# Moving the output stores to SyncE, spreading the second attention and loading batch 2 earlier, in a retention and MLP kernel

## The chip, the cores and the metric

The kernel runs on one core of a Trainium2 chip. The metric is device microseconds of a whole execution. Times are medians of several executions; the span, which the profile gives, is some 2 us shorter than the time of its execution. All profiled executions are in the fast state. The record marks one other execution of e12 and three of the kernel before beside it as slow (over 1.5% above the fastest of their kernel); the ratios leave these out. Executions of one kernel lie within some 2% of each other, so a single span can be off by as much.

Engine names as in the profile: PE is TensorE, DVE VectorE, ACT ScalarE, POOL GpSimd, SP or SPq SyncE and its queue. "DMA share" is the mean busy share of the core's 16 DMA engines. In these profiles it can pass 1 (1.41 in the kernel before, from 84.26 to 92.58 us). The granted PE clock is the share of full clock that PE was given, 1 for all of it.

## The reference

```python
scores = (q @ k.T) / sqrt(64)                 # q, k, v: 8 batches, 8 heads, 576 tokens, 64
ret = scores * Dmat                           # Dmat[h, i, j] = gamma_h ** (i - j) for i >= j, else 0
x = heads_side_by_side(ret @ v)               # 8 x 576 x 512
u = x + (x.T @ U @ V).T                       # U: 576 x 32, V: 32 x 576
out = u + relu(u @ w1) @ w2                   # w1: 512 x 2048, w2: 2048 x 512
```

## The kernel before

Two batches form a pair of nine chunks of 128 tokens; the fifth chunk (XC) is shared by the two batches. A batch goes through a "front" (load, cast, transpose, attention, mixer) and an MLP of two matmul stages, y1 and y2. In the profile, `psc` are the attention scores, `qT` and `kT` the transposed q and k, `ut` a tile of mixed tokens that goes into the MLP, `uT` its transpose, and `o_sb` a finished output tile. The program is one list of instructions, sorted by an estimate of PE's time: the front of a later batch is laid between the MLP matmuls of an earlier one. Each engine has its own part of the list, and in the trace of this kernel it works that off in order: a store on ACT was issued at 174.26 us, after the landing of a v load at 174.19, and the relu behind it, which PE had waited for 3.2 us, came at 174.85.

SyncE issues all loads of q, k, v and x and all transposes by DMA, in that order of the program. ACT does copies and relus, and in this kernel it also issues the output stores:

```python
    STQ = nc.scalar
    # ... (load of k and v for one chunk; kv_f has 4 buffers)
    f = stage.tile([P, 2, H, D], FP32, tag="kv_f", name="kv_f", bufs=4)
    for j, dram in ((0, k), (1, v)):
        nc.sync.dma_start(
            out=f[:, j], in_=dram[g, :, t0:t0 + P, :].rearrange("h s d -> s h d")
        )
    # ... (end of y2 of one tile of 128 tokens; o_sb has 3 buffers, J = 4, P = 128)
    o_sb = osb_pool.tile([P, dm], FP32, tag="o_sb", name="o_sb")
    nc.vector.tensor_tensor(out=o_sb, in0=self.ps[i], in1=self.st["u", c], op=ALU.add)
    row0 = (self.p * NCH + c) * P
    dst = out_flat[row0:row0 + P, :]
    if c != XC:
        dst = dst.rearrange("(p j) d -> j p d", j=J)
    stores.append(lambda: STQ.dma_start(out=dst, in_=o_sb))
    if len(stores) > 1:
        stores.pop(0)()
```

Two things in it matter later. A store is emitted one tile late, when the next tile's addition has been emitted. And, except for the XC tile, the rows of `o_sb` are a permutation of the tokens (token 4p+j lies in partition 32j+p), so the destination of the store is written as three nested dimensions: 4 values of j, 32 of p, 512 elements.

Of the kernel before, what the change touches and what calls it, by code (L numbers as in the profile page):

```python
# [11 lines left out]
AF = mybir.ActivationFunctionType  # L12
# [29 lines left out]
def kernel(  # L42
# [11 lines left out]
    nc = tc.nc  # L54
# [4 lines left out]
    R = moe_U.shape[1]  # L59
    P = 128  # L60
    HALF = 64
    NHP = H // 2
# [14 lines left out]
    NG = B  # L77
    AHEAD = 2
    SKEW = 0.65
    FILL1 = (0.33, 0.85)  # L80
    LOAD2 = (0.75, 0.12)
    FRONT2 = 0.15
    LAG = 2
    WARM = (4, 2, 2, 2, 2, 2)

    STQ = nc.scalar
    scale = 1.0 / math.sqrt(D)
    lng = [math.log(1.0 - 2.0 ** (-5.0 - h)) for h in range(H)]
    out_flat = out.rearrange("b s d -> (b s) d")
# [22 lines left out]
    def big(name, dtype=FP32, shape=None):  # L112
        return ps_big.tile(shape or [P, 512], dtype, tag="ps_big", name=name)
# [106 lines left out]
    def put_u(par):  # L220

        f, t, m0 = ((U_fA, U_A, 0), (U_fB, U_B, 1))[par]
        un = mix_pool.tile([P, 4, R], BF16, tag="un", name="un")
        nc.vector.tensor_copy(out=un, in_=f[:, m0:m0 + 4, :])
        ps = big("psu")
        nc.tensor.matmul(
            ps[:, 0:4 * R], perm, un.rearrange("p m r -> p (m r)"), start=True, stop=True
        )
        nc.vector.tensor_copy(
            out=t[:, m0:m0 + 4, 0:R],  # L230
            in_=ps[:, 0:4 * R].rearrange("p (m r) -> p m r", r=R),
        )

    def put_mixer_a():
        put_u(0)
        nc.vector.tensor_copy(out=U_A[0:HALF, 4, 0:R], in_=U_fA[0:HALF, 4, :])
        put_v(V_A, 0, 0)

    def put_mixer_b():
        put_u(1)  # L240
        nc.vector.tensor_copy(out=V_A[0:R, 4 * P:S], in_=V_nat[:, 4 * P:S])
        nc.vector.tensor_copy(out=U_B[HALF:P, 0, 0:R], in_=U_fB[HALF:P, 0, :])
        put_v(V_B, P, HALF)
        nc.vector.tensor_copy(out=V_B[0:R, HALF:P], in_=V_nat[:, 0:HALF])
# [8 lines left out]
    def load_w1(fbs):  # L253
        dmas = []
        for fb in fbs:
            cols = slice(fb * W1B, (fb + 1) * W1B)
            dmas.append(
                nc.gpsimd.dma_start(
                    out=w1_sb[:, :, cols],
                    in_=moe_w_ch1[:, cols].rearrange("(c p) f -> p c f", p=P),  # L260
                )
            )
        return dmas[-1]
# [51 lines left out]
            )  # L315
        sts[p]["kv_f", m + 5 * par] = f

    def cast_kv(g, m):
        cast_v(g, m)
        cast_k(g, m)  # L320

    def cast_v(g, m):
        p, c = g // 2, m + 5 * (g % 2)
# [2 lines left out]
        scale_v(t[:, 1], f[:, 1], c)  # L326
        sts[p]["k", c], sts[p]["v", c] = t[:, 0], t[:, 1]

    def cast_k(g, m):
        st, c = sts[g // 2], m + 5 * (g % 2)  # L330
        nc.vector.tensor_copy(out=st["k", c], in_=st["kv_f", c][:, 0])  # L331

    def load_x(p, part=None):

# [13 lines left out]
    def cast_x(p, part=None):  # L348
        cast_xv(p, part)
        cast_xqk(p, part)  # L350
# [16 lines left out]

    def cast_xqk(p, part=None):
        f, rows = sts[p]["x_f"], x_rows(part)
        nc.vector.tensor_copy(out=sts[p]["x3"][rows, 0:2], in_=f[rows, 0:2])  # L370

    def pair_cols(t, hp):
        return t[:, 2 * hp:2 * hp + 2, :].rearrange("p h d -> p (h d)")
# [2 lines left out]
    class Front:  # L376
# [57 lines left out]
        def TX(self, n=128):  # L434
            t = self.st["qk", XC]
            xT = x3_pool.tile([P, 2, NHP, P], BF16, tag="xT", name="xT")
            self.st["xT"] = xT
            if not self.pe_t:
                nc.sync.dma_start_transpose(
                    out=xT.rearrange("p j hp i -> p (j hp) i"),  # L440
                    in_=t.rearrange("p j h d -> p (j h d)"),
                )
                return
            ps = big("psx", BF16, [P, 2, NHP, P])
            for j in (1, 0):
                for hp in range(NHP):
                    nc.tensor.transpose(
                        ps[:, j, hp, 0:n], pair_cols(t[0:n, j], hp), ident[0:n, 0:n]
                    )
            if self.quick:  # L450
                self.copy(xT[:, 1, :, 0:n], ps[:, 1, :, 0:n])
                self.copy(xT[:, 0, :, 0:n], ps[:, 0, :, 0:n], act=False)
            else:
                self.copy(xT, ps)

# [292 lines left out]
    def first_front():  # L748
        fr = Front(0, True, quick=True)
        st = fr.st  # L750
        dummy = big("dummy")

        def warm(n):

            for _ in range(n):
                nc.tensor.matmul(
                    dummy.rearrange("p (a b) -> p a b", b=P), ident,
                    ident[:, None, :].to_broadcast([P, 4, P]), start=True, stop=True,
                )

        warm(WARM[0])
        cast_q(0, quick=True)
        cast_kv(0, 0)
        fr.TQ()
        fr.TK(0)
        cast_kv(0, 1)
        fr.SC(0)
        fr.ST(0)
        warm(WARM[1])
        fr.TK(1)  # L770
        fr.RV(0)
        cast_kv(0, 2)
        fr.SC(1)
        fr.ST(1)
        warm(WARM[2])
        fr.TK(2)
        fr.RV(1)
        put_mixer_a()
        w1a = load_w1(range(0, 2))
        cast_x(0, 0)  # L780
        fr.SC(2)
        fr.ST(2)
        fr.MA(0)
        warm(WARM[3])
        fr.TX(HALF)
        fr.RV(2)
        fr.MA(1)
        cast_kv(0, 3)
        load_w1(range(2, 4))
        fr.SC(XC, HALF, None)  # L790
        warm(WARM[4])
        fr.TK(3)
        fr.MA(2)
        fr.ST(3)
        fr.SC(3, cross=None)
        fr.CR(XC, HALF)
        fr.RV(XC, HALF, rows=slice(0, HALF))
        fr.uT_tile()
        uT = st["uT", 0]
        acc = [  # L800
            ps_s.tile([P, 512], FP32, tag="ps_s", name="uT_s"), big("uT_b"),
            big("uT_c"),
            ps_sc.tile([P, 2, 512], FP32, tag="ps_sc", name="uT_sc")[:, 0, :],
        ]

        def x_t(c, ccs=range(NCC)):
            for cc in ccs:
                nc.tensor.matmul(
                    acc[cc][:, c * P:(c + 1) * P],
                    st["x", c][:, cc * P:(cc + 1) * P], ident,  # L810
                    start=(c == 0), stop=False, skip_group_check=True,
                )

        for c in range(3):
            x_t(c, range(3))
        fr.CR(3)
        fr.RV(3)
        fr.MA(4, 3)
        for c in range(3):
            x_t(c, range(3, 4))  # L820
        fr.MA(3, 3)
        x_t(3)
        for cc in range(NCC):
            nc.tensor.matmul(
                acc[cc], st["a_sb", 0][:, cc * P:(cc + 1) * P], V_A[:, 0:4 * P],
                start=False, stop=True, skip_group_check=True,
            )
            fr.copy(uT[:, cc, :], acc[cc], act=cc % 2 == 1)
        return fr, w1a


    def loads_of(g):

        if g >= NG:
            return []
        ld = [(load_q, g)] + [(load_kv, g, m) for m in range(4)]
        cs = [(cast_q, g)] + [(cast_kv, g, m) for m in range(4)]
        if g % 2 == 0:
            ld.append((load_x, g // 2))
            cs.append((cast_x, g // 2))  # L840
        n = len(ld)
        steps = []
        for i in range(n + LAG):
            def step(i=i):
                if i >= LAG:
                    f = cs[i - LAG]
                    f[0](*f[1:])
                if i < n:
                    f = ld[i]
                    return f[0](*f[1:])  # L850
            steps.append((step,))
        return steps

    with tc.manual_schedule(engines={PE, POOL, SPQ, DVE, ACT}):
# [22 lines left out]
        for m in range(4):  # L877
# [3 lines left out]
                cast_xv(0, 1)  # L881
            if m == 2:
                w2_part = load_w2()
        fill = [(0, put_mixer_b)] + [(216, lambda c=c: first.MH(c)) for c in range(2)]
        fill += [(0, lambda: cast_k(1, 0)), (0, lambda: cast_xqk(0, 1))]
        fill += [(0, lambda: cast_q(1, (0, 1))), (0, lambda: cast_q(1, (2, 3)))]
        fill += [(216, lambda c=c: first.MH(c)) for c in range(2, 4)]
        casts = [(cast_k, 1, m) for m in range(1, 4)]
        fill += Front(1, True).items(casts, x_alone=True)

# [4 lines left out]
        def spread(items, lo, hi):  # L895
            tot = sum(c for c, _ in items) or len(items)
            at = 0.0
            for c, f in items:
                events.append((lo + (hi - lo) * at / tot, f))
                at += c if tot != len(items) else 1  # L900
# [10 lines left out]
        def at(g, share):  # L911
            return starts[g] + share * (starts[g + 1] - starts[g])

        spread(fill, at(0, FILL1[0]), at(0, FILL1[1]))
        lo2 = [(0, f) for f, in loads_of(2)]

        def first_load(f=lo2[0][1]):
            tc.add_manual_dep(f().ins, w2_part.ins.name, SYNC)

        lo2[0] = (0, first_load)  # L920
        spread(lo2, at(0, LOAD2[0]), at(1, LOAD2[1]))
        lo = at(1, FRONT2)
        fronts = {g: Front(g, False) for g in range(2, NG)}
        for g in range(2, NG):
# [37 lines left out]
```

## Time and profile before

| | before |
|---|---|
| time | 371.01 us (368.33 to 373.85) |
| span of the profiled run (an execution of 373.52 us) | 371.7 us |
| PE busy | 332.2 us, 89% |
| first y1 / first y2 | 31.18 / 59.70 us |
| first scores of batch 2 | 92.58 us |
| from there to the end of the span | 279.1 us |

The profiled execution took 2.5 us more than the median, so spans of other kernels look that much better beside it. I split the span at the first scores of batch 2, because up to there the kernel fills its pipeline, and after it the same pattern runs batch after batch.

One more reading of this kernel is needed below. It is the busy time in stretches (columns: stretch, length, then PE, weight loads, DVE, ACT, POOL, granted PE clock, DMA share, GB/s), in the tail, when all work is done and only the last store is under way:

```profile
364.80:365.80 1.00, 0.00 (x0) 0.00 (x0) 0.00 (x0) 0.00 (x0) 0.00 (x0) 1.00 0.26 100
```

This store, which has the whole machine to itself, moves 100 GB/s and keeps 0.26 of 16, so about four, DMA engines busy. I overlooked this line when I predicted.

### The profile page before, as it was taken

The page shows a single profiled execution, that of the slowest core. Times are in us where ns is not written, and L with a number is a line of the kernel's source. Part 1 is how long each engine was busy: PE and PEld are TensorE (multiplying, and loading weights), DVE is VectorE, ACT ScalarE, POOL GpSimd, SP SyncE. Part 2 cuts the span into 40 slices and gives each one's busy share as a digit, 9 for nine tenths or more (in the row PEclk, how much of TensorE's full clock was granted, in tenths as well). Part 3 has the DMA queues.
Part 4 walks back from the last instruction along what each step waited for, and adds up shares of the span by engine and source line. Part 5 has one row for each costly group of instructions (what it writes and reads, how often), then busy time and mean ns, then how long its engine had stood idle before and what let it go on. Part 6 is the DMA issues. An engine that isn't in the chain of part 4 may idle for free.

```text
span 371.7 us, 6390 instructions
## 1 busy us (share of the span) xinstructions
PE 332.2 (89%) x2606; PEld 184.4 (50%) x2642; DVE 154.8 (42%) x245; ACT 146.2 (39%) x284; POOL 56.2 (15%) x81
## 2 busy tenths in 40 slices
PE   3778687898997999996999999998999999999991
PEld 1454244445663554444665554545765544467540
DVE  5672546652853661463412662264424532210020
ACT  3425453135553126512574135504662156148200
POOL 8640620310130111112112001201100000000000
PEclk9989969999999999999899999999999999999997
DMA  8999899939999999988994347999902200110112
GB/s 208 194 200 243 175 176 266 203 83 180 192 173 222 167 118 178 212 131 168 159 212 91 78 110 157 218 112 159 112 15 67 56 23 0 50 65 2 56 48 64
DMA packets 127149, 49.66 MB, mean 134 GB/s; under 512 B 110192, under 2 KB 122480, under 8 KB 127120
## 3 DMA queue, kind: packets, MB, share of 16 engines
q1 hardware_dynamic: 117440, 35.48, 58.9%
q10 hardware_dynamic: 5456, 9.59, 9.1%
q0 software_dynamic: 4224, 4.19, 7.1%
q8 instruction: 20, 0.33, 0.5%
q14 instruction: 9, 0.07, 0.1%
HBM read 36.92 MB, written 9.44 MB: 125 GB/s over the span
## 4 chain that ended last, share of the span: by engine, by line
PE 67%; DMA 13%; SPq 7%; DVE 6%; ACT 3%; issue 2%; ACTq 0%; POOL 0%; DVEq 0%; POOLq 0%
DMA kv_f<-in_v_dram 5%; DMA kT<-kv 4%; PE psc L487 3%; SPq L313 3%; PE po L535 2%; DVE q_bf L299 2%; PE pu L600 2%; PE ph L581 2%; DMA q_f<-in_q_dram 2%; PE pss L465 2%; DVE ret L523 2%; SPq L401 2%; SPq L340 1%; PE psa L564 1%; DMA x_f<-in_v_dram 1%
## 5 line engine op out<-in xcount | busy, mean ns | idle before, releaser
L699 PEld LDWEIGHTS <-w_sb 128*128 128x128 bf16 x768 | 73.0, 99 | 52.7 <-issue 7.4
L303 POOL TENSOR_TENSOR kv<-kv_f,vscale 128x512 bf16<-128x512 f32 x32 | 34.3, 1071 | 190.4 <-DMA kv_f<-in_v_dram 133.6
L523 DVE TENSOR_TENSOR ret<-psc,tri 128x1024 bf16<-128x1024 f32 x32 | 39.1, 1223 | 33.0 <-PE psc L487 32.9
L470 ACT ACTIVATE s_sb<-pss 128x512 bf16<-128x512 f32 x32 | 19.1, 596 | 61.1 <-PE pss L465 36.1
L587 DVE TENSOR_TENSOR ut<-ph,xt 128x512 bf16<-128x512 f32 x36 | 24.4, 688 | 44.8 <-PE ph L581 44.8
L543 DVE TENSOR_TENSOR xt<-po,qscale 128x512 bf16<-128x512 f32 (+1 forms) x37 | 25.5, 689 | 21.1 <-PE po L535 20.9
L388 ACT ACTIVATE uT<-pu 128x512 bf16<-128x512 bf16 x32 | 18.9, 596 | 25.8 <-PE pu L600 21.3
L535 PEld LDWEIGHTS <-ret 128*128 128x128 bf16 x288 | 12.7, 100 | 10.5 <-DVE ret L523 5.9
L331 DVE CAST kv<-kv_f 128x512 bf16<-128x512 f32 x32 | 14.6, 462 | 4.2 <-DMA kv_f<-in_k_dram 4.1
L487 PE MATMUL psc<-qT,kT 64*128 64x128 bf16 x256 | 13.4, 227 | 2.9 <-DMA kT<-kv 1.7
L487 PEld LDWEIGHTS <-kT 64*128 64x128 bf16 x256 | 7.6, 97 | 15.5 <-issue 11.2
L600 PEld LDWEIGHTS <-ut 128*128 128x128 bf16 x128 | 9.6, 98 | 11.1 <-issue 3.2
L600 PE MATMUL pu<-ident,ut 128*128 128x128 bf16 x128 | 12.4, 219 | 3.0 <-ACT uT L388 2.6
L535 PE MATMUL po<-kv,ret 128*128 128x64 bf16 x256 | 13.2, 196 | 1.7 <-DVE ret L523 1.4
L299 DVE CAST q_bf<-q_f 128x512 bf16<-128x512 f32 x30 | 13.4, 509 | 3.0 <-DMA q_f<-in_q_dram 3.0
L709 PEld LDWEIGHTS <-y_4028 128*128 128x128 bf16 x80 | 7.8, 98 | 9.3
L465 PE MATMUL pss<-kv 128*128 128x128 bf16 x112 | 11.5, 229 | 0.8 <-ACT s_sb L470 0.7
L465 PEld LDWEIGHTS <-kv 128*128 128x128 bf16 x112 | 8.8, 102 | 5.9 <-issue 1.0
L410 PE MATMUL psq<-ident,q_bf 128*128 128x128 bf16 x32 | 4.1, 308 | 7.7 <-DVE q_bf L299 7.6
L709 PEld LDWEIGHTS <-y_1084 128*128 128x128 bf16 x80 | 7.2, 98 | 6.7
L709 PEld LDWEIGHTS <-y_3202 128*128 128x128 bf16 x80 | 7.2, 98 | 6.6
L709 PEld LDWEIGHTS <-y_2209 128*128 128x128 bf16 x80 | 7.2, 98 | 6.6
(585 smaller groups left out, 590.4 us busy)
## 6 DMA issues: line engine op xcount, KB each, us to landing
out_dram<-o_sb ACTq DMA_DIRECT2D x36, 256.0 KB
q_f<-in_q_dram SPq DMA_DIRECT2D x8, 1024.0 KB
kv_f<-in_k_dram SPq DMA_DIRECT2D x32, 256.0 KB
kv_f<-in_v_dram SPq DMA_DIRECT2D x32, 256.0 KB
w_sb<-in_moe_w_ch_dram POOLq DMA_DIRECT2D x8, 512.0 KB, 8.3
x_f<-in_k_dram SPq DMA_DIRECT2D x8, 128.0 KB
x_f<-in_q_dram SPq DMA_DIRECT2D x8, 128.0 KB
x_f<-in_v_dram SPq DMA_DIRECT2D x8, 128.0 KB
```

The source lines that it names most:

```text
L299: nc.vector.tensor_copy(out=dst, in_=src)
L303: nc.gpsimd.tensor_tensor(out=dst[rows], in0=src[rows], in1=vscale[rows, c, :, None].to_broadcast([n, H, D]), op=ALU.mult,)
L465: nc.tensor.matmul(pss[:, hp, :], pair_cols(st["k", c], hp), pair_cols(vt, hp), start=(first and hp == 0), stop=True, skip_group_check=True,)
L470: nc.scalar.activation(out=s_sb, in_=pss, func=AF.Copy)
L487: nc.tensor.matmul(psc[0:n, hl, hp, 0:n], kT[pb:pb + HALF, hp, 0:n], qTv[pb:pb + HALF, hp, 0:n], start=True, stop=True,)
L523: nc.vector.tensor_tensor(out=ret[0:n].rearrange("p (hp hl) i -> p hl hp i", hl=2)[:, :, :, 0:n], in0=psc[0:n, :, :, 0:n], in1=mask[0:n, N ...
L535: nc.tensor.matmul(po[0:n, hl, hp * D:(hp + 1) * D], ret[:, h, 0:n], vt[:, h, :], start=((c == 0 or not cross) and hp == 0), stop=True, sk ...
L543: nc.vector.tensor_tensor(out=st["x", c][rows].rearrange("p (hp hl d) -> p hl hp d", hl=2, d=D), in0=po[rows, :, 0:NHP * D].rearrange("p h ...
L587: nc.vector.tensor_tensor(out=ut, in0=ph, in1=st["x", c], op=ALU.add)
L600: nc.tensor.transpose(pu[:, cc, :], self.st["u", c][:, cc * P:(cc + 1) * P], ident)
L699: nc.tensor.matmul(ps[:, 0:n], w1_sb[:, cc, f * P:(f + 1) * P], uT[:, cc, t0:t0 + n], start=(cc == 0), stop=(cc == NCC - 1),)
L709: nc.tensor.matmul(self.ps[i], self.y1[:, f, i * P:(i + 1) * P], w2_sb[:, f, :], start=(f == 0), stop=(f == NF - 1),)
```

## The change

Its intent: shorten the start (casts of k and x on ACT), fill PE's idle time in the first y1 with the second attention, load batch 2 in one go ahead of the first store, and take the stores off ACT, whose relus had waited behind them. The core of the diff, with cuts marked:

```diff
-    FILL1 = (0.33, 0.85)
-    LOAD2 = (0.75, 0.12)
-    FRONT2 = 0.15
+    FILL1 = (0.2, 0.8)
+    LOAD2 = 0.62
+    CAST2 = (0.78, 0.12)
+    FRONT2 = 0.2
-    STQ = nc.scalar
+    STQ = nc.sync
 ... (put_u is split: its cast comes early, its matmul and copy later)
+        if quick:
+            nc.scalar.activation(out=st["k", c], in_=st["kv_f", c][:, 0], func=AF.Copy)
 ... (the same for batch 0's x cast and one xT copy; first_front reordered)
-        fill = [(0, put_mixer_b)] + [(216, lambda c=c: first.MH(c)) for c in range(2)]
-        fill += [(0, lambda: cast_k(1, 0)), (0, lambda: cast_xqk(0, 1))]
+        fill = [(216, lambda c=c: first.MH(c)) for c in range(2)]
         fill += [(0, lambda: cast_q(1, (0, 1))), (0, lambda: cast_q(1, (2, 3)))]
         fill += [(216, lambda c=c: first.MH(c)) for c in range(2, 4)]
+        fill += [(0, lambda: cast_k(1, 0)), (0, lambda: cast_xqk(0, 1))]
 ...
+        events.append((at(0, 0.05), put_mixer_b))
...
-        spread(lo2, at(0, LOAD2[0]), at(1, LOAD2[1]))
+        def load_2():
+            i = load_q(2)
+            tc.add_manual_dep(i.ins, w2_part.ins.name, SYNC)
+            for m in range(4):
+                load_kv(2, m)
+            load_x(1)
+
+        events.append((at(0, LOAD2), load_2))
+        cast_2 = [lambda hp=hp: cast_q(2, (hp,)) for hp in range(NHP)]
+        cast_2 += [lambda m=m: cast_kv(2, m) for m in range(4)] + [lambda: cast_x(1)]
+        spread([(0, f) for f in cast_2], at(0, CAST2[0]), at(1, CAST2[1]))
```

More of the change, by code (lines that the diff above doesn't have):

```diff
@@ L224, in put_u, with rest, put_mixer_a @@
         nc.vector.tensor_copy(out=un, in_=f[:, m0:m0 + 4, :])
-        ps = big("psu")
-        nc.tensor.matmul(
-            ps[:, 0:4 * R], perm, un.rearrange("p m r -> p (m r)"), start=True, stop=True
-        )
-        nc.vector.tensor_copy(
-            out=t[:, m0:m0 + 4, 0:R],
-            in_=ps[:, 0:4 * R].rearrange("p (m r) -> p m r", r=R),
-        )
-    def put_mixer_a():
-        put_u(0)
+        def rest():
+            ps = big("psu")
+            nc.tensor.matmul(
+                ps[:, 0:4 * R], perm, un.rearrange("p m r -> p (m r)"),
+                start=True, stop=True,
+            )
+            nc.vector.tensor_copy(
+                out=t[:, m0:m0 + 4, 0:R],
+                in_=ps[:, 0:4 * R].rearrange("p (m r) -> p m r", r=R),
+            )
+        return rest
+    def put_mixer_a(u_rest):
+        u_rest()
         nc.vector.tensor_copy(out=U_A[0:HALF, 4, 0:R], in_=U_fA[0:HALF, 4, :])
@@ L239, in put_mixer_b @@
     def put_mixer_b():
-        put_u(1)
+        put_u(1)()
         nc.vector.tensor_copy(out=V_A[0:R, 4 * P:S], in_=V_nat[:, 4 * P:S])
@@ L316, in load_kv, with cast_kv @@
         sts[p]["kv_f", m + 5 * par] = f
-    def cast_kv(g, m):
+    def cast_kv(g, m, quick=False):
         cast_v(g, m)
-        cast_k(g, m)
+        cast_k(g, m, quick)
     def cast_v(g, m):
@@ L327, in cast_v, with cast_k @@
         sts[p]["k", c], sts[p]["v", c] = t[:, 0], t[:, 1]
-    def cast_k(g, m):
+    def cast_k(g, m, quick=False):
         st, c = sts[g // 2], m + 5 * (g % 2)
-        nc.vector.tensor_copy(out=st["k", c], in_=st["kv_f", c][:, 0])
+        if quick:
+            nc.scalar.activation(out=st["k", c], in_=st["kv_f", c][:, 0], func=AF.Copy)
+        else:
+            nc.vector.tensor_copy(out=st["k", c], in_=st["kv_f", c][:, 0])
     def load_x(p, part=None):
@@ L369, in cast_xqk @@
         f, rows = sts[p]["x_f"], x_rows(part)
-        nc.vector.tensor_copy(out=sts[p]["x3"][rows, 0:2], in_=f[rows, 0:2])
+        dst, src = sts[p]["x3"][rows, 0:2], f[rows, 0:2]
+        if part == 0:
+            nc.scalar.activation(out=dst, in_=src, func=AF.Copy)
+        else:
+            nc.vector.tensor_copy(out=dst, in_=src)
     def pair_cols(t, hp):
@@ L451, in TX @@
                 self.copy(xT[:, 1, :, 0:n], ps[:, 1, :, 0:n])
-                self.copy(xT[:, 0, :, 0:n], ps[:, 0, :, 0:n], act=False)
+                self.copy(xT[:, 0, :, 0:n], ps[:, 0, :, 0:n])
             else:
@@ L764, in first_front @@
         fr.TQ()
+        u_rest = put_u(0)
         fr.TK(0)
-        cast_kv(0, 1)
+        cast_kv(0, 1, True)
         fr.SC(0)
+        put_mixer_a(u_rest)
         fr.ST(0)
@@ L771, in first_front @@
         fr.RV(0)
-        cast_kv(0, 2)
+        cast_kv(0, 2, True)
         fr.SC(1)
@@ L777, in first_front @@
         fr.RV(1)
-        put_mixer_a()
         w1a = load_w1(range(0, 2))
@@ L782, in first_front @@
         fr.ST(2)
+        cast_kv(0, 3, True)
+        load_w1(range(2, 4))
         fr.MA(0)
+        fr.TX(HALF)
         warm(WARM[3])
-        fr.TX(HALF)
         fr.RV(2)
         fr.MA(1)
-        cast_kv(0, 3)
-        load_w1(range(2, 4))
         fr.SC(XC, HALF, None)
-        warm(WARM[4])
         fr.TK(3)
         fr.MA(2)
+        fr.SC(3, cross=None)
         fr.ST(3)
-        fr.SC(3, cross=None)
         fr.CR(XC, HALF)
@@ L912, in at @@
             return starts[g] + share * (starts[g + 1] - starts[g])
+        events.append((at(0, 0.05), put_mixer_b))
         spread(fill, at(0, FILL1[0]), at(0, FILL1[1]))
-        lo2 = [(0, f) for f, in loads_of(2)]
-        def first_load(f=lo2[0][1]):
-            tc.add_manual_dep(f().ins, w2_part.ins.name, SYNC)
-        lo2[0] = (0, first_load)
-        spread(lo2, at(0, LOAD2[0]), at(1, LOAD2[1]))
+        def load_2():
[8 more added lines that the diff above has]
+        spread([(0, f) for f in cast_2], at(0, CAST2[0]), at(1, CAST2[1]))
         lo = at(1, FRONT2)
```

## The prediction

> **What bounds the kernel now.** I read the page first. TensorE (PE) is busy 332.2 of 371.7 us, and no other engine passes 42%. So a change can only win what PE idles, 39.5 us, and what it runs at a lowered clock. Next I asked for the busy time of each engine in stretches cut at the events that matter: first matmul of the first y1 (31.18), first y2 (59.70), first y1 of batch 1 (84.26), first scores of batch 2 (92.58), the end of the last matmul (364.1).
>
> ```profile
> 0.00:31.18 31.18, 19.59 (x204) 11.90 (x207) 18.73 (x40) 10.15 (x18) 17.77 (x42) 0.95 1.17 212
> 31.18:59.70 28.52, 21.24 (x123) 10.32 (x125) 12.53 (x21) 14.19 (x24) 8.43 (x9) 0.88 1.03 197
> 59.70:84.26 24.56, 22.45 (x208) 11.36 (x210) 14.68 (x23) 6.81 (x12) 5.82 (x6) 1.00 0.82 173
> 84.26:92.58 8.32, 6.57 (x49) 4.42 (x47) 2.54 (x5) 5.08 (x12) 0.00 (x0) 1.00 1.41 163
> 92.58:170.00 77.42, 74.18 (x633) 40.17 (x644) 40.08 (x63) 29.57 (x57) 11.47 (x12) 1.00 1.03 172
> 170.00:180.00 10.00, 6.78 (x59) 4.60 (x56) 2.82 (x4) 3.78 (x9) 2.68 (x3) 0.83 1.02 166
> 180.00:364.10 184.10, 181.37 (x1344) 101.59 (x1360) 62.76 (x92) 76.59 (x156) 9.99 (x10) 1.00 0.50 89
> ```
>
> Columns: stretch, length, busy time of PE, weight loads, DVE, ACT, POOL, granted PE clock, DMA share, GB/s. PE idles 11.6 us before the first y1, 7.3 to the first y2, 2.1 and 1.8 in the next two, 3.2 in each of the two up to 180, 2.7 afterwards, 7.6 in the tail (last addition, last store). The DMA share is at or above 1 from the start to 180, except in 59.7 to 84.3. So two things compete for the first 92 us: a chain of PE, DVE and ACT, and the transfers.
>
> The waits of PE name the engines:
>
> ```profile
> PE psq L410 <- DVE q_bf L299: 7.6, 3, 4.7
> PE ps_y_2228 L699 <- ACT y_2209 L703: 3.2, 1, 3.2
> PE po L535 <- DVE ret L523: 2.8, 4, 1.3
> PE pu L600 <- ACT uT L388: 2.6, 2, 2.2
> PE psc L487 <- DMA kT<-kv: 1.7, 1, 1.7
> ```
>
> (us, times, longest.) The second and fourth rows are ACT held up, not ACT busy. The chain of waits shows by what:
>
> ```profile
> 168.86 5.33 DMA kv_f<-in_v_dram
> 174.26 0.55 ACTq L724
> 174.85 0.45 ACT y_2209 L703
> 175.34 0.70 PE ps_y_2228 L699 x4
> ```
>
> L724 is the store of an output tile, on ACT's queue. [...] a store waits for a k/v load; the relu behind it in ACT's order waits too, and PE runs out of PSUM. The same happens at 118.22 (2.2 us) and 254.85 (1.2 us).
>
> [...] 110192 of 127149 packets are under 512 B; k/v loading runs at about 205 GB/s (52 to 57 us), the q load with its longer runs at 320 (83 to 85 us). [...] a cast of k on DVE took 1.17 us at 15.25, beside a POOL multiply, against a median of 0.42; on ACT the same shape from f32 took 0.61 to 0.63. [...] the clock halves. The trace agrees: 0.50 from 47.5 to 52.5 us after the idle there, and y1 matmuls of 634 ns instead of 379.
>
> **The change part by part.**
>
> *Start.* Three k casts (0.42 to 1.17 each), the x cast (0.67) and one xT copy (0.29) leave DVE for ACT, which has 21 us idle there. The U/V preparation comes earlier and no longer stops PE between RV(1) and SC(2) (the wait of 1.0 for "un"), and two of twelve dummy matmuls go. Walking the order through with the old durations: mask of chunk 1 at 15.4 (was 16.34), scores of chunk 2 at 17.6 (19.23), scores of chunk 3 at 22.2 (25.22), then the unchanged tail of some 6 us plus 0.4, as ST(3) now follows SC(3). First y1 at about 28.5, so 2.7 us earlier.
>
> *Second attention from a fifth of the first y1.* Before, 12 y1 groups ran, then PE stood idle until DVE had done U_B, V_B, two ut, k, x and four q casts (41.2 to 49.2; the casts 0.83 each). Now the mixer's copies run at 0.05, where DVE is idle, and q is cast straight after two ut, at about 36.3; q's load was issued at 25.55 and must have landed by about 35, as the v load after it landed at 37.22. The idle of 5.2 us in 40 to 50 shrinks to about 1.5, and the half clock of about 5 us (2.5 us lost) mostly goes. The last four y1 groups now sit between attention steps. First y2 at about 50 to 51 (was 59.7), with two chunks of attention (about 1.15 us of PE each) more done by then; end of batch 0 at about 73 to 74 (was 84.26). Block 1 of w2 landed at 53.7 (its completion let the load of q(2) go), about when its first matmul would come: a wait of 0 to 2 us.
>
> That would be 10 us, but the transfers don't follow.
>
> *Batch 2's load.* Its q load is still tied to w2's second block, w2's issue on POOL still to the v casts of batch 1, and those to loads that run at the DMA's rate. So it still starts near 53.7 and its x lands near 76.4, as before. What goes is the hole after it: DMA share 0.2 in 75 to 80 us, while DVE reached the q cast at 79.03 and the first transpose went at 80.96. Now casts come earlier and the queue goes on at once with three stores (0.79 MB, about 2.4 us at 320 GB/s), q(3) (1.05 MB, 3.3 us) and the transposes (the first kT landed about 7 us after q(3) had drained). The sum is 76.4+2.4+3.3+7 = 89; part of the stores may overlap the loads, so 88.
>
> ```profile
> 82.61 9.93 DMA kT<-kv
> 92.58 0.42 PE psc L487 x8
> ```
>
> So scores of batch 2 start at 88 instead of 92.58: **4.5 us gained**, not 10. PE waits some 5 us there instead of 1.7, either at kT or because the addition of the last tile of batch 0 waits for the first store (three o_sb buffers) and keeps its PSUM bank.
>
> *Stores on SyncE.* The three stops of ACT go: 2.2+3.2+1.2 = 6.6 us, plus about 1.3 us for the half clock after 175.3 (y1 groups 1.05 us apart instead of 0.54 for four groups, less one). I give back 1.4 us, as transposes and loads now stand behind stores in SyncE's order: **6.5 us gained**. Each store is emitted one tile late, so its data is there when SyncE reaches it, and transposes are issued two steps ahead.
>
> Sum: 371.0 - 4.5 - 6.5 = 360.0 us.
>
> **Rivals.** (a) *PE's chain binds the first 92 us, not the DMA.* For it: the biggest PE wait is on DVE, and DMA has holes at 45 and 75 us. Against it: the load of batch 2 hangs on w2, which this change doesn't bring forward. Then the whole 10 us stay, and the time is about 354. (b) *The first part is fully hidden behind transfers, or paid back as a cold clock.* For it: loads at a share above 1 up to 45 us[...]. Then only the ACT stops are won: about 365. (c) *SyncE becomes the bound:* a store waiting for its addition holds back transposes. Against it: SyncE's issue times in 100 to 180 leave gaps, and third-chunk transposes come some 6 us ahead of need. If it bit once per batch with 1.5 us, six batches give 9 us back: about 369. (d) *w2 late for the first y2:* at most 2 us more, and probably hidden by the wait for kT: 360 to 361.
>
> **Range and chances.** My weights are about one half for the sum, a quarter for (a), a fifth for (b), the rest for (c). The three times of before span 368.3 to 373.9, so the ratio has some 0.5% of noise. Range 354 to 367. The 2% line is 363.6; the sum lies 1% beyond it, so faster 0.74, same 0.24, slower 0.02.
>
> **What would show each step.** First y1 near 28.5 us. Idle of PE before the first transposes of batch 1 below 2 us and no stretch at 0.5 clock near 47 to 52. First y2 near 50, end of batch 0 near 74. Batch 2's q load still issued near 53, DMA share near 1 from 53 to 90 without a hole, and batch 2's first scores near 88 after a wait of several us for a transpose or a PSUM bank. No PE wait on a relu or uT copy of ACT over 1 us after 100 us. Wrong if: w2's second block lands much before 53; PE waits on kT in later batches; SyncE waits on o_sb additions pass on to PE.

## The result, and the profile after

The changed kernel took **385.74 us** (383.18 to 386.32), the kernel before, with one more execution, 372.43 us (368.33 to 374.51). The ratio is 1.0382, with a 95% interval of 1.027 to 1.0494: slower by 3.8%, where I had predicted 3% faster. Ratios here are those of the record, which are worked out from the fast runs alone, so they are not quite the ratios of the medians.

The busy time in stretches, cut at the same events as before (first y1, first y2, first y1 of batch 1, first scores of batch 2), and finer after them:

```profile
0.00:28.39 28.39, 18.13 (x205) 11.54 (x205) 16.60 (x35) 12.91 (x23) 16.89 (x42) 1.00 1.20 204
...
74.42:89.69 15.27, 9.99 (x63) 6.28 (x61) 2.97 (x6) 6.50 (x15) 1.65 (x2) 0.89 0.91 151
...
130.00:150.00 20.00, 17.11 (x98) 7.49 (x95) 4.76 (x8) 8.25 (x14) 2.91 (x3) 0.91 0.51 113
150.00:160.00 10.00, 5.56 (x20) 2.55 (x21) 2.58 (x4) 2.27 (x4) 1.65 (x2) 0.66 1.31 197
...
230.00:250.00 20.00, 12.17 (x52) 5.35 (x51) 3.70 (x6) 6.34 (x11) 2.70 (x3) 0.74 0.91 148
```

The start went as hoped: first y1 at 28.39, first y2 at 50.69, end of batch 0 at 74.42 us. Then PE idles 5.3 us, and batch 2's first scores come at 89.69, only 2.9 us earlier than before. From there to the end the changed kernel needs 294.0 us where the old one needed 279.1: 14.9 us lost (in one execution of each). The rows show where: around 150 and 240 us PE stands, and then runs at a granted clock of 0.66 and 0.74. PE's waits (us, times, longest) name it:

```profile
PE pu L613 <- DVE ut L600: 13.2, 2, 7.7
PE ps_y_1101 L712 <- DVE o_sb L730: 3.5, 1, 3.5
```

The chain of waits (start, duration, what; the longest pieces) through the first of the two:

```profile
126.72 0.70 DVE o_sb L730
127.42 0.23 SPq L737
...
128.29 9.73 DMA kv_f<-in_v_dram
...
138.84 7.72 DMA kv_f<-in_k_dram
...
149.72 3.25 DMA x_f<-in_q_dram
...
153.70 0.69 DVE ut L600
...
155.05 1.71 PE ps_y_1955 L712 x4
```

Read it from the end. PE runs a y1 group in 1.71 us, against 0.86 us at full clock. It had waited for `ut` of DVE; DVE has the x cast ahead of `ut` in its order, and stood for the x load. That load was issued late, because SyncE was behind a chain of k and v loads that took 9.73 and 7.72 us each. In this piece the chain begins with a store (L737) released by its addition, and the loads just behind it are the slow ones. And all the while the DMA share is only 0.51: the queue crawls while the DMA engines seem half idle.

My **first theory (1)**: SyncE, in order, stands at stores until their additions are done, so loads come late. **Rival 1**: the new places of the fronts do the harm, and the stores have nothing to do with it.

### The profile page after: what moved, and what is told of

Read it like the earlier page. It is cut to its first block, busy times and chain, and to the rows that moved or that the text cites. A ratio compares the mean times of both kernels' runs of the same rounds, so it can differ in the third digit from the quotient of the medians.

```text
span 383.7 us, 6420 instructions
## 1 busy us (share of the span) xinstructions
PE 338.0 (88%) x2640; PEld 185.3 (48%) x2640; DVE 153.9 (40%) x240; ACT 149.3 (39%) x289; POOL 55.7 (15%) x81
## 4 chain that ended last, share of the span: by engine, by line
PE 57%; DMA 23%; SPq 13%; DVE 2%; issue 1%; POOL 1%; ACT 0%; DVEq 0%; POOLq 0%
DMA kv_f<-in_v_dram 8%; SPq L319 8%; DMA kv_f<-in_k_dram 5%; DMA w_sb<-in_moe_w_ch_dram 5%; SPq L349 3%; DMA x_f<-in_q_dram 2%; PE pu L613 2%; PE psc L500 2%; DMA out_dram<-o_sb 2%; DMA kT<-kv 2%; PE ph L594 1%; PE po L548 1%; PE pss L478 1%; PE psa L577 1%; PE ps_y_1680 L722 1%
## 5 line engine op out<-in xcount | busy, mean ns | idle before, releaser
L712 PEld LDWEIGHTS <-w_sb 128*128 128x128 bf16 x768 | 74.0, 101 | 53.2 <-issue 10.3
L613 PE MATMUL pu<-ident,ut 128*128 128x128 bf16 x128 | 13.3, 230 | 13.7 <-DVE ut L600 13.2
L340 DVE CAST kv<-kv_f 128x512 bf16<-128x512 f32 x29 | 15.6, 540 | 21.6 <-DMA kv_f<-in_k_dram 20.6
L548 PEld LDWEIGHTS <-ret 128*128 128x128 bf16 x288 | 13.1, 100 | 9.4 <-DVE ret L536 4.4
L500 PE MATMUL psc<-qT,kT 64*128 64x128 bf16 x256 | 13.1, 224 | 3.6 <-ACT kT L401 1.9
L523 PE MATMUL po<-s_sb,qT 64*128 64x64 bf16 x224 | 8.0, 191 | 2.8 <-DVE xt L556 2.8
```

The source lines that it names most:

```text
L500: nc.tensor.matmul(psc[0:n, hl, hp, 0:n], kT[pb:pb + HALF, hp, 0:n], qTv[pb:pb + HALF, hp, 0:n], start=True, stop=True,)
L548: nc.tensor.matmul(po[0:n, hl, hp * D:(hp + 1) * D], ret[:, h, 0:n], vt[:, h, :], start=((c == 0 or not cross) and hp == 0), stop=True, sk ...
L613: nc.tensor.transpose(pu[:, cc, :], self.st["u", c][:, cc * P:(cc + 1) * P], ident)
L712: nc.tensor.matmul(ps[:, 0:n], w1_sb[:, cc, f * P:(f + 1) * P], uT[:, cc, t0:t0 + n], start=(cc == 0), stop=(cc == NCC - 1),)
```

## The experiments

All have three rounds of timing against the kernel before, which ran beside them on the same chip: e1 to e3 on one chip, e4 to e7 on a second, e8 to e11 on a third, e12 on a fourth. The medians of the kernel before there were 371.54, 371.16, 372.29 and 371.93 us, so a comparison across groups can be off by about 1 us. The table below gives all results at once; "first scores" are those of batch 2, and "rest" is the span minus that, both of the one profiled execution. "Wrong" marks a run that gives a wrong result on purpose.

| run | stores on | store's form | median us | ratio (95%) | first scores | rest |
|---|---|---|---|---|---|---|
| before | ACT | 4x32 rows | 371.0 | 1 | 92.58 | 279.1 |
| after | SyncE | 4x32 rows | 385.74 | 1.038 (1.027 to 1.049) | 89.69 | 294.0 |
| e1, after | ACT | 4x32 rows | 367.80 | 0.989 (0.984 to 0.994) | 89.81 | 276.8 |
| e2, before | SyncE | 4x32 rows | 402.72 | 1.082 (1.078 to 1.087) | 109.98 | 291.0 |
| e3, after | GpSimd | 4x32 rows | 374.74 | 1.007 (1.001 to 1.012) | 89.43 | 283.8 |
| e4, after, wrong | SyncE | zeros, 4x32 rows | 369.85 | 0.995 (0.988 to 1.002) | 90.34 | 278.0 |
| e5, after, wrong | SyncE | one row | 352.68 | 0.949 (0.942 to 0.955) | 84.17 | 267.4 |
| e6, after | SyncE, two tiles late | 4x32 rows | 373.25 | 1.005 (0.997 to 1.013) | 86.25 | 284.0 |
| e7, after | GpSimd, two tiles late | 4x32 rows | 374.47 | 1.005 (0.997 to 1.013) | 86.93 | 282.1 |
| e8, after, wrong | SyncE | 128 plain rows | 354.45 | 0.953 (0.946 to 0.959) | 83.70 | 267.4 |
| e9, after, wrong | ACT | 128 plain rows | 354.94 | 0.954 (0.947 to 0.961) | 85.13 | 266.6 |
| e10, after | SyncE | four of 32 rows | **357.59** | 0.960 (0.953 to 0.968) | 85.98 | 270.9 |
| e11, after | ACT | four of 32 rows | 364.03 | 0.978 (0.971 to 0.986) | 91.41 | 268.5 |
| e12, before | SyncE | four of 32 rows | 376.48 | 1.010 (0.995 to 1.025) | 104.00 | 270.6 |

### e1: the changed kernel, stores back on ACT

```diff
-    STQ = nc.sync
+    STQ = nc.scalar
```

> The changed kernel with the stores alone put back on ACT's queue. Theory 1 (the stores in SyncE's in-order queue hold up the k/v and x loads behind them; the other parts of the change gain the 2.9 us seen at batch 2's first scores): 366 to 371 us, ratio to before 0.985 to 0.997, waits of PE for 'ut' back under 1 us in all, ACT stops of 2 to 3 us back. Rival 1 (the new places of the second attention and of batch 2's front do the harm, whoever issues the stores): 380 us or more, with the waits for 'ut' of 5 and 7 us still there.

It took 367.80 us, ratio 0.9889. The rest fell from 294.0 to 276.8 us. So the queue of the stores alone accounts for about 18 us, and rival 1 is out. The ACT stops are back, as expected. This is one, from ACT's timeline:

```profile
172.09 0.55 ACTq L737 DMA_DIRECT2D out_dram<-o_sb  x1
172.68 1.67 ACT L716 ACTIVATE y<-ps_y 128x320 bf16<-128x320 f32 x4 [1.83 <-DMA kv_f<-in_v_dram]
```

The bracket is the idle time before the relu and what ended it: the landing of a v load, for which the store ahead of it had waited.

### e2: the kernel before, stores on SyncE

```diff
-    STQ = nc.scalar
+    STQ = nc.sync
```

> The kernel before with the stores alone moved to SyncE. Theory 1: 383 to 389 us (ratio 1.03 to 1.045), PE waiting for 'ut' and x for more than 8 us in all. Rival 1, and my prediction's own step: the three stops of ACT (6.6 us) go and little comes back, 365 to 369 us (ratio 0.98 to 0.99).

It took 402.72 us, so the direction of theory 1 holds and its size doesn't: 31 us lost. The rest is 291.0 us, like that of the changed kernel. The other 17 us lie ahead of batch 2's scores, where PE waited 13.1 us for `kT`; e12 comes back to this.

### e3: stores on GpSimd

```diff
-    STQ = nc.sync
+    STQ = nc.gpsimd
```

> The changed kernel with the stores on GpSimd's queue[...]. Theory 1 expects neither ACT nor SyncE to be held: 362 to 366 us (ratio 0.972 to 0.985). Rival: GpSimd, which scales v in order, now stands for each o_sb addition, so the v casts come late and kv_f buffers come free late: 370 to 385 us. Rival 1: 380 or more.

At 374.74 us, theory 1's range was missed by 9 us; the time lies in that of the rival on GpSimd's order. PE waited 5.8 us for `kT` and 4.0 for `ut`, though neither ACT nor SyncE was held by a store. e7 tests the rival's reason.

### e4 and e5: the wait without the bytes, the bytes without the wait

Both give a wrong result on purpose. In e4 the store writes a tile of zeros, ready from the start:

```diff
-    V_nat = consts.tile([R, S], FP32, name="V_nat")
+    V_nat = y1_pool.tile([R, S], FP32, tag="y11", name="V_nat")
+    z_st = consts.tile([P, dm], FP32, name="z_st")
...
+        nc.gpsimd.memset(z_st, 0.0)
...
-            stores.append(lambda: STQ.dma_start(out=dst, in_=o_sb))
+            stores.append(lambda: STQ.dma_start(out=dst, in_=z_st))
```

> Wrong on purpose: the changed kernel with the same 36 stores at the same places of SyncE's queue, but each writes a tile of zeros that is ready from the start, so SyncE never waits for an addition, while the same bytes and the same number of issues stay in its queue. (V_nat lies in memory of a later y1 tile, to make room.) Theory 1a, the wait for o_sb is what holds the loads: 360 to 367 us (ratio 0.968 to 0.985), waits of PE for 'ut' under 1.5 us. Theory 1b, the place of the bytes in the same queue ahead of loads and transposes is what costs: 376 to 386 us, and the waits for 'ut' of several us stay.

In e5 the store waits for its `o_sb` but writes one row:

```diff
-            stores.append(lambda: STQ.dma_start(out=dst, in_=o_sb))
+            stores.append(lambda: STQ.dma_start(out=out_flat[row0:row0 + 1, :], in_=o_sb[0:1]))
```

> Wrong on purpose, the counterpart: each store writes one row of 2 KB of its o_sb in place of 128, so SyncE waits for each addition as in the changed kernel, but the bytes are gone. Theory 1a: 378 to 386 us (ratio 1.015 to 1.04), waits for 'ut' of 5 to 8 us stay; the wait of 3.5 us for the first store at 76 us shortens. Theory 1b: 358 to 367 us.

e5 took 352.68 us with its waits for `o_sb` in place, below even the range of theory 1b. That refutes theory 1a: in this order of the program, the waits alone cost nothing. e4 took 369.85 us, between the two forecasts, and the waits that matter stayed, as its PE waits and its stretch at the same place show:

```profile
PE pu L615 <- DVE ut L602: 9.6, 1, 9.6
```
```profile
140.00:150.00 10.00, 6.29 (x29) 2.56 (x27) 0.43 (x1) 4.35 (x8) 1.49 (x2) 1.00 0.55 111
```

SyncE waited for no addition there, and still the loads crawled at a DMA share of 0.55. So the bytes cost, but not as a load on all 16 DMA engines: these are on average half idle. Taking away the wait made the harm smaller (one stop instead of two), taking away the bytes removed it.

### e6 and e7: the stores two tiles late

```diff
-    osb_pool = ctx.enter_context(tc.tile_pool(name="osb_pool", bufs=3))
+    osb_pool = ctx.enter_context(tc.tile_pool(name="osb_pool", bufs=4))
-            if len(stores) > 1:
+            if len(stores) > 2:
 ... (V_nat moved as in e4; in e7 also STQ = nc.gpsimd)
```

> The changed kernel, correct, stores on SyncE but emitted two tiles late instead of one, with four o_sb buffers (V_nat lies in memory of a later y1 tile, to make room). Theory 1a: SyncE may run one tile of y2 (some 4 to 6 us) further ahead of PE, which halves the loss: 368 to 376 us. Theory 1b: 380 to 386 us.

> The same with the stores on GpSimd. If GpSimd's v casts behind the waiting stores were what cost the GpSimd variant its gain (waits for kT 5.8 and for 'ut' 4.0 us), both shrink by more than half: 361 to 368 us (ratio 0.97 to 0.99). [...] nothing moves: 372 to 377 us.

e6 took 373.25 us: it helps by 12 us, as theory 1a said it would, but one wait for `ut` of 9.0 us stays, as in e4. e7 took 374.47 us, as before the delay. The waits on `kT` and `ut` did shrink (5.8 to 3.9, 4.0 to 2.1), with nothing gained, so the rival's reason isn't it. The last store of e3, alone in the tail, moved 86 GB/s at a share of 0.26, like the one below, so this form too keeps about four engines busy; I didn't try it with other stores, and how much of its time that explains stays open.

**Theory 2.** The tail of the kernel before gave it away: a store by itself uses about 4 of 16 DMA engines (share 0.26) and moves 100 GB/s. At that rate the 262 KB take 2.6 us of each of the four. The slowest dimension of the store's destination, 4x32x512, is 4 as well. Loads have a slowest dimension of 128 on both sides, and where the q load runs (83 to 85 us in the kernel before) the share is 0.98, at 324 GB/s. So my guess, which no run had shown yet, was that the 4 in the store's shape keeps it on four engines, and that every load and transpose issued behind the store on its queue then stands behind it on those four, while the other twelve idle.

The kept trace of the changed kernel agrees with it. In the crawl, between 131 and 133 us, with the v load of 128.29 issued and not landed until 138.03, the queue moved this:

```profile
DMA packets 92, 0.18 MB, mean 91 GB/s; under 512 B 3, under 2 KB 3, under 8 KB 92
q1 hardware_dynamic: 92, 0.18, 25.4%
```

Only rows of stores have packets of 2 KB in this trace (4608, which is 36 x 128), so for 2 us it moved almost nothing but the two stores (89 of 92 packets), at a quarter of the engines' time. The trace also keeps the increments of the DMAs' semaphores, though no view prints them. In the changed kernel 32 of the 36 stores make five, for the first store below one at 127.45 us and four from 131.70 to 133.35; the four XC stores, and every load and transpose, make 16. The profile puts the landing of the v load at 138.03, the time of its last increment. I read each of the 16, and each of a store's last four, as one engine's share that has landed; the trace doesn't say so. Here are the times (us) around the first pair of stores in the crawl, and at the same place in e8, which comes next:

| | issued | twelfth increment | last four increments |
|---|---|---|---|
| changed kernel, store | 126.39 | none | 131.70 to 133.35 |
| changed kernel, k load | 127.74 | 131.01 | 135.69 to 137.12 |
| changed kernel, v load | 128.29 | 135.41 | 136.59 to 138.03 |
| e8, store | 117.47 | 121.11 | 121.15 to 121.29 |
| e8, k load | 118.96 | 123.04 | 123.06 to 123.20 |
| e8, v load | 119.40 | 124.26 | 124.28 to 124.32 |

Twelve shares of the k load were there at 131.01, and four came 5 to 6 us later, after the last increment of the first store (133.35). Over the whole run, the last share of a k or v load came up to 6.8 us after its twelfth in the changed kernel, and at most 1.8 us in e8 and 1.7 us in e10.

### e8 and e9: the same bytes, on all engines

Wrong on purpose: the rows go out in plain order, so the slowest dimension is 128 on both sides. Bytes, data packets, waits and places in the queue stay. (The page of e8 counts 384 more packets under 512 B, twelve for each of 32 stores: its last store, alone in the tail, has 16 of them, the last four of the changed kernel have 4 each.)

```diff
             dst = out_flat[row0:row0 + P, :]
-            if c != XC:
-                dst = dst.rearrange("(p j) d -> j p d", j=J)
```

> Wrong on purpose: the changed kernel, stores on SyncE, one tile late, each waiting for its own addition, same bytes and same 2 KB packets; only the order of the rows in DRAM is the plain one, so the store's slowest dimension is 128 in place of 4. Theory 2 (a store with a slowest dimension of 4 runs on 4 of the 16 DMA engines and takes about 2.6 us of each, and the loads and transposes issued behind it on the same queue stand behind it on those four): the harm goes although waits and bytes stay, 354 to 364 us (ratio 0.95 to 0.98), waits for 'ut' under 1.5 us. Theory 1 in both forms (the wait for o_sb, or the bytes as such): 378 to 388 us.

> Wrong on purpose: as the run before, but the stores on ACT. Theory 2: [...] spreading the store still gains, 357 to 366 us, and SyncE may now be the better queue for it by some us, since the stops of ACT stay. Theory 1: unchanged from the run with stores on ACT, 366 to 369 us.

e8 took 354.45 us: 31 us less than the changed kernel, from the shape of one access pattern. (The order of the rows in DRAM changed too; e10 keeps the old order and is as good but for 3 us, so the order isn't what cost.) Its last store, alone in the tail:

```profile
349.00:349.50 0.50, 0.00 (x0) 0.00 (x0) 0.00 (x0) 0.00 (x0) 0.00 (x0) 1.00 0.89 344
```

That is 344 GB/s at a share of 0.89, against 100 at 0.26. The same piece of SyncE's timeline (start, duration, what), from the pair of stores to the x load, first in the changed kernel, then in e8:

```profile
126.39 1.26 SPq L737 DMA_DIRECT2D out_dram<-o_sb  x2
127.74 0.50 SPq L319 DMA_DIRECT2D kv_f<-in_k_dram  x1
128.29 4.47 SPq L319 DMA_DIRECT2D kv_f<-in_v_dram  x1
132.85 3.97 SPq L414 DMA_TRANSPOSE qT<-q_bf  x1
...
140.05 6.21 SPq L414 DMA_TRANSPOSE qT<-q_bf  x1
...
147.62 0.70 SPq L349 DMA_DIRECT2D x_f<-in_k_dram  x1
```
```profile
117.47 1.39 SPq L735 DMA_DIRECT2D out_dram<-o_sb  x2
118.96 0.39 SPq L319 DMA_DIRECT2D kv_f<-in_k_dram  x1
119.40 1.19 SPq L319 DMA_DIRECT2D kv_f<-in_v_dram  x1
120.68 1.88 SPq L414 DMA_TRANSPOSE qT<-q_bf  x1
...
126.91 1.59 SPq L414 DMA_TRANSPOSE qT<-q_bf  x1
...
129.86 1.33 SPq L349 DMA_DIRECT2D x_f<-in_k_dram  x2
```

The same work takes SyncE 21.2 us in the one and 12.4 in the other, and the issues that took 4 to 6 us take 1 to 2.

e9, on ACT, took 354.94 us, the same as e8, and 2 us below its range; my forecast that SyncE might then be the better queue by some us was wrong. With one store a tile on 16 engines it made 0.5 us of difference which of the two queues carried it. With 4 it mattered by 18 us (e1 against the changed kernel). Even on ACT's own queue the four-engine form cost 13 us (e1 against e9).

The rests part this further. The four-engine form costs 10.2 us on ACT (e1 less e9), 10.6 us on SyncE when no store waits for its addition (e4 less e8), and 26.6 us on SyncE when they do wait (changed kernel less e8); the waits without the form cost nothing (e5 has the same rest as e8). So most of the 18 us between the queues is the form and the waits together. The likely reason, argued and not shown, is that a SyncE that stands at stores loses the lead that would hide slow loads.

### e10 and e11: a correct form

The permutation can be kept if each store is cut into four of 32 rows, each with a slowest dimension of 32:

```diff
-            stores.append(lambda: STQ.dma_start(out=dst, in_=o_sb))
+            def store():
+                if c == XC:
+                    STQ.dma_start(out=dst, in_=o_sb)
+                    return
+                for j in range(J):
+                    STQ.dma_start(out=dst[j], in_=o_sb[j * PJ:(j + 1) * PJ])
+
+            stores.append(store)
```

> A correct form of the same: the changed kernel, each store of 128 permuted rows cut into four of 32 rows, so each has a slowest dimension of 32, on SyncE. Theory 2: 356 to 370 us; better than the changed kernel by over 4%, but worse than the plain-row run by the 96 more issues of some 0.5 us in SyncE's order[...]. Theory 1: 386 us or worse.

> The same four stores of 32 rows on ACT, correct. Theory 2: 358 to 370 us; ACT pays four issues of some 0.5 us a tile[...]. Theory 1: 367 us or worse.

e10, on SyncE, is correct and took **357.59 us**, ratio 0.960: it beats both kernels, and it loses only 3 us to e8 for 96 more issues. The stretch in which the changed kernel crawled has PE busy and a DMA share of 0.89 again:

```profile
130.00:150.00 20.00, 19.19 (x121) 9.29 (x121) 7.26 (x10) 11.12 (x19) 3.73 (x4) 1.00 0.89 195
```

e11, on ACT (the change in STQ as in e1 besides), took 364.03 us. Its rest, 268.5, is as good, but up to batch 2's scores PE waited once 6.0 us for a `uT` copy of ACT. So with four stores a tile the queue does matter: SyncE is 6.4 us faster.

### e12: the kernel before with e10's stores

The diff of e10 on the kernel before, with STQ on SyncE.

> The kernel before with its stores on SyncE, each cut into four of 32 rows; nothing else of the change. Theory 2: the harm that SyncE did to it (402.7 us) goes with the four-engine stores, and the ACT stops stay away: 362 to 369 us (ratio 0.975 to 0.99); the distance to 357.6 us of the changed kernel with the same stores, some 4 to 11 us, is what the other parts of the change are worth once stores no longer hold the loads. Rival: in the order of before, batch 2's loads are spread between batch 0's stores, which then wait for PE, so that SyncE still holds the x loads: 375 us or more, with the wait for kT of 13 us mostly there.

At 376.48 us (376.38 without the slow execution) the rival was right. The rest, 270.6 us, equals that of e10 (270.9). The whole difference between the two lies ahead of batch 2's scores, 104.00 against 85.98 us. Here SyncE's timeline and PE's wait show why:

```profile
73.25 1.77 SPq L730 DMA_DIRECT2D out_dram<-o_sb  x4
75.11 0.40 SPq L282 DMA_DIRECT2D q_f<-in_q_dram  x1
```
```profile
PE psc L487 <- DMA kT<-kv: 12.0, 1, 12.0
```

In the order of before, the first store stands ahead of batch 2's q load. SyncE waits for the first output tile until 73 us, and the q load goes out at 75.11 instead of 54.05 (in the changed kernel) or 53.72 (before, where ACT had the store). So loading batch 2 ahead of the first store is what stores on SyncE need; these two parts of the change belong together. This is the one place that I found, here and in e2, where a wait for `o_sb` by itself held the loads.

## Why the prediction was wrong

**The start and the second attention: right.** First y1 at 28.39 us (predicted 28.5), first y2 at 50.69 (50 to 51), end of batch 0 at 74.42 (73 to 74). PE waited 0.8 us for the first transposes of batch 1, and no stretch near 50 us ran at half clock (the granted clock was 1.00 from 28.39 to 74.42 us).

**Batch 2's load: the mechanism right, two terms mis-sized.** The q load was issued at 54.05 (predicted 53.7), and both waits that I named came: 3.5 us because `o_sb` of the last tile of batch 0 waited for the first store, and 1.7 us for `kT`. First scores came at 89.69 in place of 88, and that this is so near is luck. One term that failed is "three stores (0.79 MB, about 2.4 us at 320 GB/s)". I took the q load's rate for a store. By itself a store runs at 100 GB/s, so three take 7.9 us of four engines: 5.5 us more. e8, in which only this is mended, has its first scores at 83.70, 6.0 us earlier than the changed kernel. The other is the 7 us from the end of the q load to the first kT. By the increments, the last share of that load landed at 88.60 and kT at 89.64, so 1.0 us (and 88.88 and 92.54, or 3.7 us, in the old trace). The two errors cancelled.

**"I give back 1.4 us, as transposes and loads now stand behind stores in SyncE's order": this step failed.** It credited 7.9 us for the ACT stops and debited 1.4. The stops did go: no wait of PE on a relu or `uT` copy passed 1 us after 100 us. But the rest grew by 14.9 us, so the debit was about 22.8 (against e1, which has the ACT stops still, the rest grew by 17.2). I had looked for gaps in SyncE's issue times, which exist, and at whether a store's data is ready, which it nearly always was: between 89 and 160 us SyncE waited 3.3 us in all for additions. I hadn't asked how long a store occupies the engines that the next load needs. I had taken it, with no run to show it, that a store takes as long from either queue, so that the move would only free ACT. That fits e8 and e9, where the queue is indifferent (354.45 and 354.94 us), and fails for four-engine stores (385.74 us on SyncE, 367.80 on ACT). With the stores cut in four (e10 and e12) the rest is 270.6 to 270.9 us, 8.2 to 8.5 us better than before: about what this step promised. But that agreement is luck as well. Some 2 us of it may be the long execution of before, and e9, with the stores still on ACT, has a rest of 266.6 us and after 90 us no wait of PE for ACT over 0.7 us. So the ACT stops that I wanted to buy off go with the four-engine stores too, without moving the stores: the right change here was to their form, and not to their queue.

**Rival (c), "SyncE becomes the bound", was the true one, and came by another road.** I gave it what was left of the weights, at most one twentieth, and 369 us. A store waiting for its addition wasn't the main thing (e5); it made the four-engine store worse (e4 against the changed kernel: 16 us of the rest).

**Rival (a), that PE's chain and not the DMA binds the first 92 us**, made 354 us. e8 came to 354.45 us, with first scores 8.9 us earlier than before. What I took for a bound by the DMA's rate there was in part the slow stores. That the totals agree is chance: (a) left the stores out.

**Three readings of the old trace were wrong**, none of which moved the sum. The 5.2 us between 40 and 50 us are PE's busy time (5.23); its idle time there was 4.8. The 205 GB/s at 52 to 57 us were not k and v: from 54.5 to 57 us all 520 packets were of w2's queue (q0). From 62 to 67 us, where k and v load, it was 210, so the figure stands by luck. And at 118.22 the store had waited for a transpose, not for a k or v load.

What stays open: an increment in the trace doesn't name its engine, so that the four late shares and the store lie on the same four engines is read from counts and times. Why the waits make the four-engine form worse is argued. And how much of the time of the GpSimd form (e3, e7) its four-engine stores explain wasn't tried.

## What to carry to other kernels

Before you move a DMA to another queue, look at one of its kind by itself in the trace: GB/s and DMA share together tell how many engines it uses (here 100 GB/s at 0.26, against 344 at 0.89). A transfer on four of sixteen engines held up the transfers queued behind it (21.2 us of SyncE's timeline for what took 12.4 in e8), and a mean DMA share of one half (0.51), with stretches near one quarter (0.25), while the queue crawled was its mark; giving it a slowest dimension of 32 or 128 in place of 4 was worth 7 to 8% here with the stores on SyncE, and 1% (four stores a tile) to 3.5% (one store) on ACT; all the rest of the change, without it, was worth 1% (e1). On a queue that works its list off in order, as SyncE did here, put the loads of the next stage ahead of the first store that waits for this one: in e12 the q load behind that store went out at 75.11 us, in the changed kernel, ahead of it, at 54.05.
